# Batch 1's K and Q through TensorE, batch 0's MLP input through TensorE, W2 behind V, and one token-mixing step for a tile shared by two batches

## The chip, the cores and the metric

The kernel runs on one core of a Trainium2 chip. The metric is device time in microseconds (us), the median of several executions. The engines of the core each work through their own instructions in order: TensorE (PE, with its weight loads shown as PEld), VectorE (DVE), ScalarE (ACT), GpSimd (POOL) and SyncE (SP, which here only issues DMAs). They wait for each other and for DMAs by semaphores.

## What is computed

Attention over 8 batches, 8 heads, 576 positions and head size 64, with a mask that keeps a window of 32 positions either side and 8 global positions; then a two-step MLP block over 512 channels.

```
scores = scale * q @ k^T            (masked: |i-j| <= 32, or i or j global)
attn   = softmax(scores);  x = attn @ v          x as [8, 576, 512]
a1  = alpha1 * x + beta1
u   = x + lam * (w_tok @ a1)                     mixes the 576 positions
a2  = alpha2 * u + beta2
out = u + lam * (relu(a2 @ w_ch1) @ w_ch2)       hidden size 2048
```

## The kernel before

**Tiling.** Each batch has 576 = 4.5 x 128 positions. The MLP works on a flat list of 36 tiles of 128 rows over all batches, so every even batch ends in the upper half of a flat tile, and the next odd batch starts in its lower half (`flat_rows`, L270: tile u = 4 of an even batch and u = 0 of an odd one are the same flat tile f). The MLP takes four flat tiles at a time, as group g of 9.

**Stages of a batch.** `qk` (L278) makes transposed window scores from KTz (K transposed, zero padded per head) and QT (Q transposed), exponentiates on ACT and masks on DVE into PTz and GRT. `pg` (L324) does the global rows, `xg` (L308) the global columns. `pv` (L335) multiplies with V, normalizes on DVE into x, and POOL writes XL = x * LA1. `tokmix` (L372) multiplies wtT (w_tok transposed; wtT[0] for even, wtT[1] for odd batches, shifted by 64 columns) with XL, five matmuls of 128x512 for each of five tiles u (L383); DVE adds x into the tile U[f] (L384). When a tile's 128 rows are complete, DVE multiplies by alpha2 into u16 (L390), and a DMA transpose on SP's queue puts it into UT[g] (L391), the transposed MLP input. `mlp(g)` (L447) needs the four tiles of UT[g]: 16 x 4 matmuls with W1 (L455), Relu with a bias on ACT (L458), 4 x 16 matmuls with W2 (L464), two DVE operations and the output DMA.

**Order.** The order on each engine is the order in which the program is written. Batch 0 runs alone, written out by hand at L485 to L682 (the prelude), in which weights and constants are also loaded. From batch 1 on, `front(b)` is a generator whose yields say how many MLP matmuls come between two pieces of attention: 8 MLP matmuls first, then 120 in each `front`. During `front(1)` only group 0 exists (128 matmuls), so group 1 starts right after `tokmix` of batch 1.

**K and Q.** Batch 0 loads 512 of 576 positions so that a partition holds 4 consecutive positions (`qk0_half`, L161, runs of 1 KB in memory), casts to bf16 into a scratch in HTb, and TensorE transposes (`kt`, `qt`, `rest`, L519 to L539); ACT and DVE copy from PSUM into KTz and QT. All other batches load with `qk_chunk` (L174: five chunks of 128 positions, runs of 256 bytes), cast into kz and q16, and use DMA transposes on SP's queue (`xbar_k` L186, five of them; `xbar_q` L190, two). In the prelude, batch 1's chunks are cast on ACT (`c_qk[...](SC)`), three of its `xbar_k` stand before `pv(0, 3)`, two behind `wt_sums`, and `xbar_q` inside the loop over batch 0's `tokmix` (L665).

**Weights.** w_tok comes by a POOL DMA (L572), is transposed by TensorE in `wt_tr` (L583) and completed by `wt_sums`. W1 and W2 come in four blocks each, by POOL's queue, with a cast from float32 (`w1_dma` L601, `w2_dma` L604): W1's at L622, L630, L640 and L660; W2's first two before, and its last two behind, the casts of batch 1's V.

**Buffers.** R has three tiles and RV two for float32 loads; a load waits until the cast of what lay there is done. PSUM: mm 1, ml 3, sc 2, xps 1 buffers. XL, GS, RS and wtT exist twice, by parity of the batch.

Of the kernel before, what the change touches and what calls it, by code (L numbers as in the profile page):

```python
# [31 lines left out]
def A(t, off, dims, p0=0, n=P):  # L32
    row = t.ap[0][0]
    return bass.AP(t.tensor, t.offset + p0 * row + off, [[row, n]] + dims)
# [22 lines left out]
def kernel(  # L57
# [42 lines left out]
    def ml(dtype=FP32, cols=512):  # L100
        return psL.tile([P, cols], dtype, name="ml", tag="ml")

    def sc(dtype=FP32):
        return psS.tile([P, 512], dtype, name="sc", tag="sc")

    def u_tile():
        return pU.tile([P, DM], FP32, name="U")
# [45 lines left out]
    def next_r():  # L153
        r_n[0] += 1
        return R[(r_n[0] - 1) % 3]
# [2 lines left out]
        return 1600 * (t % 2) + 320 * (t // 2)  # L158


    def qk0_half(i, hh, r):  # L161
        nc.sync.dma_start(
            out=A(r, 0, [[256, 4], [1, 256]]),
            in_=(k, q)[i][0, 4 * hh : 4 * hh + 4, 0:512, :].rearrange("h (p c) d -> p h (c d)", c=4),
        )
        return lambda E: copy(E, out=A(HTb, KQ0 + 2560 * i + 256 * hh, [[64, 4], [512, 4], [1, D]]), in_=A(r, 0, [[256, 4], [64, 4], [1, D]]))

    def qk0_rest(r):
        for i, src in enumerate((k, q)):
            nc.sync.dma_start(out=A(r, 0, [[64, 8], [1, 64]], 64 * i, 64), in_=src[0, :, 512:576, :].rearrange("h p d -> p h d"))  # L170
        return lambda E: copy(E, out=A(HTb, KQ0 + 2048, [[1, 512]]), in_=r[:, 0:512])


    def qk_chunk(b, c):  # L174
        n = P if c < 4 else 64
        r = next_r()
        for i, src in enumerate((k, q)):
            nc.sync.dma_start(out=A(r, 512 * i, [[64, 8], [1, D]], 0, n), in_=src[b, :, P * c : P * c + n, :].rearrange("h p d -> p h d"))

        def cast(E):  # L180
            copy(E, out=A(kz, 1024 * c, [[256, 4], [192, 2], [1, D]], 0, n), in_=A(r, 0, [[128, 4], [64, 2], [1, D]], 0, n))
            copy(E, out=q16[0:n, c, :], in_=r[0:n, 512:1024])

        return cast
# [36 lines left out]
    def glob_kq(kq):  # L221
        kqn = pS.tile([P, 2, D], BF16, name="kqn")
        G.tensor_tensor(out=kqn[0:64], in0=A(kq, 0, [[0, 2], [1, D]], 0, 64), in1=A(cst, C_PAR, [[1, 2], [0, D]], 0, 64), op=ALU.mult)
        G.tensor_copy(out=kqn[64:P], in_=A(kq, 0, [[0, 2], [1, D]], 64, 64))
        return kqn
# [20 lines left out]
    def masks_b(scr):  # L246
        d72, e72 = A(scr, 8, [[8, 9], [1, 8]]), A(scr, 80, [[8, 9], [1, 8]])
        V.tensor_scalar(out=notg, in0=notg, scalar1=-1.0, scalar2=1.0, op0=ALU.mult, op1=ALU.add)
        V.tensor_tensor(out=notg, in0=notg, in1=cst[:, C_VALID : C_VALID + 9], op=ALU.mult)
        V.tensor_tensor(out=mask, in0=A(cst, C_BAND, [[0, 9], [1, 64]]), in1=A(notg, 0, [[1, 9], [0, 64]]), op=ALU.mult)  # L250
        V.tensor_tensor(out=e72, in0=d72, in1=d72, op=ALU.mult)
        V.tensor_scalar(out=e72, in0=e72, scalar1=float(WIN * WIN), scalar2=None, op0=ALU.is_gt)
        V.tensor_tensor(out=grm, in0=A(scr, 80, [[16, 5], [1, 8]]), in1=A(notg, 0, [[2, 5], [0, 8]]), op=ALU.mult)
# [118 lines left out]

    def tokmix(b, x):
        par = b % 2
        for u in range(5):
            f, r0, r1 = flat_rows(b, u)
            if f not in U:
                while len(U) >= 9:
                    yield 1
                U[f] = u_tile()  # L380
            ps = sc()
            for c in range(5):
                T.matmul(out=ps, lhsT=wtT[par][:, c, P * u : P * u + P], rhs=XL[par][:, c, :], start=(c == 0), stop=(c == 4))  # L383
            V.tensor_tensor(out=U[f][r0:r1, :], in0=ps[r0:r1, :], in1=x[r0:r1, u, :], op=ALU.add)  # L384
            if r1 == P:
                g = f // 4
                if g not in UT:
                    UT[g] = pUT.tile([P, 4, 512], BF16, name="UT")
                u16 = pU16.tile([P, DM], BF16, name="u16")
                V.tensor_tensor(out=u16, in0=U[f], in1=a2b, op=ALU.mult)  # L390
                nc.sync.dma_start_transpose(out=UT[g][:, :, P * (f % 4) : P * (f % 4) + P], in_=u16)  # L391
            yield 4


    def front(b, kqn):
# [90 lines left out]
    nc.sync.dma_start(out=cst, in_=nc.inline_tensor(_consts(), name="cst_np").ap())  # L486
    scr, a1b, b1r, colr = u_tile(), u_tile(), u_tile(), u_tile()
    stage = [pUT.tile([P, 1024], FP32, name="UT") for _ in range(2)]
    c_k0 = qk0_half(0, 0, next_r())
    c_q0 = qk0_half(1, 0, next_r())  # L490
    c_k1 = qk0_half(0, 1, next_r())
    c_q1 = qk0_half(1, 1, stage[0])
    c_rest = qk0_rest(stage[1])

    make_identity(nc, identb)
    G.memset(dum, 0.0)
# [22 lines left out]
    def kt(p, engs):  # L519
        ps = ml(BF16)  # L520
        for c in range(4):
            T.transpose(out=ps[:, c * P : (c + 1) * P], in_=A(HTb, KQ0 + 512 * c + P * p, [[1, P]]), identity=identb)
        for hh in range(2):
            copy(engs[hh], out=A(KTz, 640 * (2 * p + hh) + 32, [[4, P], [1, 4]], 64 * hh, 64), in_=A(ps, 0, [[1, P], [P, 4]], 64 * hh, 64))

    def qt(p):
        ps = sc(BF16)
        for c in range(4):
            T.transpose(out=ps[:, c * P : (c + 1) * P], in_=A(HTb, KQ0 + 2560 + 512 * c + P * p, [[1, P]]), identity=identb)
        for e in range(2):  # L530
            SC.copy(out=A(QT, 1600 * e + 80 * p, [[320, 4], [4, 16], [1, 4]]), in_=A(ps, 16 * e, [[32, 4], [1, 16], [P, 4]]))  # L531

    def rest():
        ps = ml(BF16)
        for p in range(4):
            T.transpose(out=ps[:, P * p : P * p + P], in_=A(HTb, KQ0 + 2048 + P * p, [[1, P]]), identity=identb)
        for hh in range(2):
            V.tensor_copy(out=A(KTz, 640 * hh + 544, [[1280, 4], [1, 64]], 64 * hh, 64), in_=A(ps, 0, [[P, 4], [1, 64]], 64 * hh, 64))
        SC.copy(out=A(QT, qo(8), [[80, 4], [1, 64]]), in_=A(ps, 64, [[P, 4], [1, 64]]))  # L539
# [8 lines left out]
    with nc.allow_non_contiguous_dma(reason="column-major 512-vector load (one time)"):  # L548
        nc.sync.dma_start(out=b2c, in_=moe_beta2.rearrange("(c p) -> p c", p=P))
    kt(0, (V, V))  # L550
    masks_b(scr)
    c_q0(SC)
    qt(0)
    G.memset(ecol, 0.0)
    G.memset(A(ecol, 0, [[64, 2]]), 1.0)
    G.memset(wt16[:, :, 576:704], 0.0)
# [1 line left out]
    G.memset(ve[96:P, 4, :, 0:64], 0.0)  # L558
    c_k1(SC)
    kt(1, (V, V))  # L560
    kqn = glob_kq(kq)
    c_rest(V)
    rest()
    glob(kqn)
    c_q1(SC)
    qt(1)
    c_v[0](G)
    c_v[1](G)
    c_v[2](G)
# [7 lines left out]
    gs_init(0, colr)  # L577
    V.tensor_copy(out=A(RS[0], 64, [[65, 8]], 0, 64), in_=cst[0:64, C_BD : C_BD + 8])
    glob_v(V, 0, vg)
    c_qk = [qk_chunk(1, c) for c in range(3)]  # L580


    def wt_tr(c):  # L583
# [5 lines left out]
    def wt_sums():  # L589
        for hf in range(2):  # L590
# [3 lines left out]
            SC.copy(out=wtT[0][64:65, 4, 288 * hf : 288 * hf + 288], in_=ps[64:65, 0:288])  # L594
            SC.copy(out=wtT[1][0:1, 0, 64 + 288 * hf : 352 + 288 * hf], in_=ps[0:1, 0:288])

    def drain(gen):
        for _ in gen:
            pass

    def w1_dma(blk):  # L601
        G.dma_start(out=W1[:, :, 512 * blk : 512 * blk + 512], in_=moe_w_ch1[:, 512 * blk : 512 * blk + 512].rearrange("(c p) e -> p c e", p=P))
# [3 lines left out]

    x = pX.tile([P, 5, DM], FP32, name="x")
    drain(qk(0, 0))
    kt(2, (V, SC))
    kt(3, (V, SC))  # L610
    qt(2)
    qt(3)
    drain(qk(0, 1))
    drain(pg(0))
    V.tensor_tensor(out=LA1, in0=a1b, in1=lamb, op=ALU.mult)
    xg(0, 0)
    xg(0, 1)
    G.memset(XL[0][64:P, 4, :], 0.0)
    G.memset(wtT[1][:, :, 0:64], 0.0)
    G.memset(wtT[1][0:64, 0, 64:640], 0.0)  # L620
    G.memset(GS[1], 0.0)
    w1_dma(0)  # L622
    qk2 = qk(0, 2)
    for _ in range(3):
        next(qk2)
    pv(0, 0, x)
    drain(qk2)
    c_qk[0](SC)
    wt_tr(0)
    w1_dma(1)  # L630
    qk3 = qk(0, 3)
    for _ in range(3):
        next(qk3)
    c_qk.append(qk_chunk(1, 3))
    pv(0, 1, x)
    drain(qk3)
    xg(0, 2)
    c_qk[1](SC)
    wt_tr(1)
    w1_dma(2)  # L640
    xbar_k(0)
    c_qk.append(qk_chunk(1, 4))
    xbar_k(1)
    pv(0, 2, x)
    V.tensor_tensor(out=XL[0][64:65, 4, :], in0=b1r[64:65, :], in1=lamb[64:65, :], op=ALU.mult)
    xg(0, 3)
    wt_tr(2)
    c_qk[2](SC)
    wt_tr(3)
    xbar_k(2)  # L650
    pv(0, 3, x)
    wt_tr(4)
    wt_sums()
    c_qk[3](SC)
    c_qk[4](SC)
    xbar_k(3)
    xbar_k(4)
    V.tensor_copy(out=b2a, in_=b2c)
    kq, vg = gathers(1)
    w1_dma(3)  # L660
    G.memset(RS[1], 0.0)
    G.memset(XL[1][0:64, 0, :], 0.0)
    kqn = glob_kq(kq)
    mix = tokmix(0, x)
    for i, _ in enumerate(mix):  # L665
        if i == 1:
            xbar_q()
    glob(kqn)
    V.tensor_copy(out=A(RS[1], 64, [[65, 8]], 0, 64), in_=cst[0:64, C_BD : C_BD + 8])
    glob_v(V, 1, vg)  # L670
    gs_init(1, colr)
    V.tensor_tensor(out=XL[1][0:1, 0, :], in0=b1r[0:1, :], in1=lamb[0:1, :], op=ALU.mult)
    w2_dma(0)
    w2_dma(1)
    c_v = [v_part(1, i) for i in range(3)]
    for c in c_v:
        c(G)
    v_shift(G)
    w2_dma(2)
    w2_dma(3)  # L680
    nc.sync.dma_start(out=A(wtT[1], 64, [[640, 5], [1, S]], 64, 64), in_=A(wtT[0], 0, [[640, 5], [1, S]], 0, 64))
    nc.sync.dma_start(out=A(wtT[1], 640 + 64, [[640, 4], [1, S]], 0, 64), in_=A(wtT[0], 0, [[640, 4], [1, S]], 64, 64))  # L682

# [55 lines left out]
```

## Time and profile before

| | |
|---|---|
| median of 14 runs | 436.28 us (431.55 to 441.60) |
| the profiled execution's own time | 432.71 us |
| its span, first to last instruction | 430.9 us |
| PE / DVE / ACT / POOL busy in the span | 87% / 52% / 39% / 42% |
| mean granted TensorE clock | 0.962 |
| DMA | 66.44 MB, mean 154 GB/s; 176067 of 189804 packets under 512 B |
| first MLP matmul (L455) | at 68.06 us |

How to read it: the profile divides the span into 40 slices of 10.8 us and gives for each engine the busy share in tenths, and the clock that TensorE was granted. A chain of work is followed back from the last instruction, at each step to what released it; it can be listed by time. A group of instructions is one line, engine, operation and tile, with the mean of one. A wait is idle time of an engine, put down to what released it. For a DMA the profile gives SP's or POOL's issue (SPq, POOLq) and the time from issue to landing. A PE matmul's duration contains its way through the array, so in a stream the start-to-start time is shorter than it: 128x512 matmuls have a mean of 388 ns, and start about 215 ns apart at full clock.

### The profile page before, as it was taken

Reading aid. Unit: us, or ns where it says so; the run is one execution under the profiler, and the core shown is the slowest. Engines: PE = TensorE matmul, PEld = TensorE weight load, DVE = VectorE, ACT = ScalarE, POOL = GpSimd, SP = SyncE. Lnnn points to the kernel's source line nnn. Section 1 sums busy time; section 2 is a strip of 40 time slices with the busy share of each in tenths; the row PEclk is TensorE's granted clock in tenths of the full one; section 3 lists DMA queues with packets and bytes.
Section 4 is the critical chain, followed back from the end, with each engine's and each line's share of the span. In section 5 each row is a group of like instructions: output and inputs, shape, how many; then the busy total and the mean of one; then the engine's idle time right before and its main releaser. Section 6 shows DMA issues by size and latency. Waiting matters only on the chain.

```text
span 430.9 us, 8312 instructions
## 1 busy us (share of the span) xinstructions
PE 375.7 (87%) x3295; PEld 208.4 (48%) x3351; DVE 223.5 (52%) x446; ACT 168.1 (39%) x293; POOL 181.7 (42%) x241
## 2 busy tenths in 40 slices
PE   1485606999779999999999999989999999999995
PEld 1374202664346545654564565446545654444442
DVE  7745440355815684559555764766385547303123
ACT  6446302750047206710770266036603740360720
POOL 7625702657643746647473657346640140000000
PEclk9998955999969999999999999999999999999999
DMA  8999999999995999888999998889883002201001
GB/s 237 200 211 220 157 198 183 211 210 161 250 203 83 144 218 220 163 159 209 215 181 181 185 223 142 181 190 220 139 195 103 14 2 86 73 2 73 24 26 73
DMA packets 189804, 66.44 MB, mean 154 GB/s; under 512 B 176067, under 2 KB 183747, under 8 KB 189765
## 3 DMA queue, kind: packets, MB, share of 16 engines
q1 hardware_dynamic: 183044, 56.93, 66.2%
q0 software_dynamic: 6720, 8.98, 11.7%
q8 instruction: 26, 0.43, 0.4%
q14 instruction: 14, 0.11, 0.1%
HBM read 39.28 MB, written 9.44 MB: 113 GB/s over the span
## 4 chain that ended last, share of the span: by engine, by line
PE 64%; DMA 11%; DVE 8%; SPq 6%; POOL 4%; issue 4%; ACT 2%; POOLq 0%; DVEq 0%
PE ml L455 26%; PE ml L464 21%; PE sc L383 5%; DMA UT<-u 4%; PE sc L285 3%; PE xps L347 3%; DMA R<-in_q_dram 3%; DMA R<-in_k_dram 2%; POOL XL L359 2%; PE xps L348 2%; DVE U L384 2%; PE mm L313 2%; PE sc L330 1%; DMA lamb<-in_moe_lam_dram 1%; SPq L192 1%
## 5 line engine op out<-in xcount | busy, mean ns | idle before, releaser
L455 PE MATMUL ml<-UT,W 128*128 128x512 bf16 x539 | 142.8, 388 | 14.2 <-DMA UT<-u 12.2
L458 ACT ACTIVATE HTb<-ml,bias1T 128x512 bf16<-128x512 f32 x144 | 99.1, 688 | 105.1 <-PE ml L455 98.3
L464 PE MATMUL ml<-W,HTb 128*128 128x512 bf16 x559 | 134.6, 379 | 0.8
L464 PEld LDWEIGHTS <-HTb 128*128 128x128 bf16 x576 | 54.5, 98 | 59.5
L455 PEld LDWEIGHTS <-W 128*128 128x128 bf16 x576 | 49.7, 100 | 54.3 <-issue 8.6
L359 POOL TENSOR_TENSOR XL<-x,LA 128x512 bf16<-128x512 f32 x32 | 42.5, 1328 | 67.0 <-DVE x L352 65.4
L469 DVE TENSOR_TENSOR tmp<-ml,lamb 128x512 f32<-128x512 f32 x36 | 24.8, 690 | 68.3 <-PE ml L464 65.9
L292 ACT ACTIVATE Pt<-sc 128x432 f16<-128x432 f32 x90 | 47.5, 528 | 14.7 <-PE sc L285 14.6
L383 PE MATMUL sc<-XL,wtT 128*128 128x512 bf16 x198 | 49.2, 379 | 1.7 <-POOL XL L359 0.8
L331 ACT ACTIVATE GS<-sc 64x320 f16<-64x320 f32 (+1 forms) x16 | 6.5, 403 | 107.5 <-PE sc L330 107.5
L110 POOL CAST ve<-RV 128x1024 f16<-128x1024 f32 x16 | 19.1, 1196 | 62.1 <-DMA RV<-in_v_dram 60.6
L285 PEld LDWEIGHTS <-KTz 128*128 128x128 bf16 x576 | 31.7, 103 | 24.4 <-issue 4.2
L390 DVE TENSOR_TENSOR u<-U,a2b 128x512 bf16<-128x512 f32 x36 | 34.0, 943 | 10.6 <-DMA UT<-u 9.4
L384 DVE TENSOR_TENSOR U<-sc,x 128x512 f32<-128x512 f32 (+1 forms) x40 | 27.4, 685 | 22.9 <-PE sc L383 22.8
L294 DVE TENSOR_TENSOR GRT<-Pt,grm 128x80 f16<-128x80 f16 x32 | 8.7, 270 | 56.2 <-ACT Pt L292 56.2
L285 PE MATMUL sc<-QT,KTz 128*128 128x72 bf16 x540 | 33.2, 201 | 4.0 <-ACT QT L531 3.4
L347 PEld LDWEIGHTS <-PTz 128*128 128x128 f16 x576 | 31.3, 100 | 9.0 <-issue 3.8
L348 PE MATMUL xps<-RS,GS 128*128 128x65 f16 x320 | 32.3, 197 | 3.6 <-DVE RS L321 3.6
L347 PE MATMUL xps<-ve,PTz 128*128 128x65 f16 x320 | 33.2, 196 | 0.3 <-DVE x L352 0.3
L383 PEld LDWEIGHTS <-wtT 128*128 128x128 bf16 x200 | 19.5, 98 | 25.5 <-issue 1.6
L347 PE MATMUL xps<-vo,PTz 128*128 128x65 f16 x256 | 30.0, 197 | 0.0
L348 PEld LDWEIGHTS <-GS 128*128 128x128 f16 x320 | 28.8, 100 | 1.9
(113 smaller groups left out, 363.5 us busy)
## 6 DMA issues: line engine op xcount, KB each, us to landing
out_dram<-U SPq DMA_DIRECT2D x36, 256.0 KB, 2.7
R<-in_k_dram SPq DMA_DIRECT2D x28, 256.0 KB, 5.1
R<-in_q_dram SPq DMA_DIRECT2D x28, 256.0 KB, 5.2
RV<-in_v_dram SPq DMA_DIRECT2D x24, 256.0 KB, 4.6
W<-in_moe_w_ch_dram POOLq DMA_DIRECT2D x8, 512.0 KB, 9.9
vo<-ve POOLq DMA_DIRECT2D x14, 260.0 KB, 4.2
RV<-in_v_dram SPq DMA_DIRECT2D x8, 192.0 KB, 4.8
R<-in_v_dram SPq DMA_DIRECT2D x8, 192.0 KB, 4.3
```

Source lines behind the costliest of these rows:

```text
L285: T.matmul(out=ps[:, i * 144 + 72 * hh : i * 144 + 72 * hh + 72], lhsT=KTz[:, 2 * p + hh, 64 * t : 64 * t + P], rhs=A(QT, qo(t) + 80 * p, ...
L292: SC.activation(out=Pt[:, 432 * un : 432 * un + 432], in_=ps[:, 0:432], func=AF.Exp, bias=0.0, scale=0.125)
L347: T.matmul(out=o_, lhsT=ptz[:, base : base + P], rhs=vv, start=(i == 0), stop=False)
L348: T.matmul(out=o_, lhsT=gs[:, P * u : P * u + P], rhs=rs[:, h, :], start=False, stop=True)
L359: G.tensor_tensor(out=A(xl, DM * full + P * p, [[DM, 4], [1, P]]), in0=A(x, DM * full + P * p, [[DM, 4], [1, P]]), in1=A(LA1, P * p, [[0, ...
L383: T.matmul(out=ps, lhsT=wtT[par][:, c, P * u : P * u + P], rhs=XL[par][:, c, :], start=(c == 0), stop=(c == 4))
L384: V.tensor_tensor(out=U[f][r0:r1, :], in0=ps[r0:r1, :], in1=x[r0:r1, u, :], op=ALU.add)
L390: V.tensor_tensor(out=u16, in0=U[f], in1=a2b, op=ALU.mult)
L455: T.matmul(out=ps, lhsT=W1[:, cc, ec * P : (ec + 1) * P], rhs=ut[:, cc, :], start=(cc == 0), stop=(cc == 3))
L458: SC.activation(out=HTb[:, slots[ec], :], in_=ps, func=AF.Relu, bias=bias1T[:, ec : ec + 1], scale=1.0)
L464: T.matmul(out=ps, lhsT=HTb[:, slots[ec], P * j : P * j + P], rhs=W2[:, ec, :], start=(ec == 0), stop=(ec == 15))
L469: V.tensor_tensor(out=tmp, in0=ps, in1=lamb, op=ALU.mult)
```

## The change

1. The loader of 1 KB runs takes the batch as an argument, and batch 1 uses it too. `qk_chunk(1, ...)`, its casts and its seven DMA transposes go; TensorE transposes with `kt`, `qt` and `rest` take their place in the prelude. ACT casts (five calls), and ACT and DVE copy from PSUM.
2. For batch 0, all `kt` and `qt` come before the first `qk(0, 0)`, and the remaining 64 positions are loaded and handled before the second half of the heads.
3. In `tokmix`, batch 0's u16 tiles go through four TensorE transposes and one DVE copy from PSUM (`ut_pe`, one tile behind), not through a DMA transpose.
4. The shared flat tile: an even batch at u = 4 only copies x into U[f]. The odd batch at u = 0 does ten matmuls with 64 weight columns each, alternating between the upper half (wtT[0], XL[0], output rows 0 to 63) and the lower half (wtT[1], XL[1], rows 64 to 127) of one PSUM tile; one more DVE addition takes the upper half into U[f].
5. W1's blocks and all four blocks of W2 are issued later: W2 behind the casts and the shift of batch 1's V. The index gathers of batch 1 move forward.

```diff
-    def qk0_half(i, hh, r):
+    def qk4_half(b, i, hh, r):
...
     def tokmix(b, x):
         par = b % 2
+        wait = []
+        def ut_pe():
+            f, u16 = wait.pop(0)
+            ps = ml(BF16)
+            for cc in range(4):
+                T.transpose(out=ps[:, cc * P : (cc + 1) * P], in_=u16[:, cc * P : (cc + 1) * P], identity=identb)
+            V.tensor_copy(out=UT[f // 4][:, :, P * (f % 4) : P * (f % 4) + P], in_=A(ps, 0, [[P, 4], [1, P]]))
         for u in range(5):
...
+            if par == 0 and u == 4:
+                V.tensor_copy(out=U[f][0:64, :], in_=x[0:64, 4, :])
+                yield 4
+                if wait:
+                    ut_pe()
+                continue
             ps = sc()
-            for c in range(5):
-                T.matmul(out=ps, lhsT=wtT[par][:, c, P * u : P * u + P], rhs=XL[par][:, c, :], start=(c == 0), stop=(c == 4))
+            if r0:
+                for c in range(5):
+                    for i, c0 in enumerate((512, 64)):
+                        T.matmul(out=ps[64 * i : 64 * i + 64, :], lhsT=wtT[i][:, c, c0 : c0 + 64], rhs=XL[i][:, c, :], start=(c == 0), stop=(c == 4))
+                V.tensor_tensor(out=U[f][0:64, :], in0=ps[0:64, :], in1=U[f][0:64, :], op=ALU.add)
+            else:
+                for c in range(5):
+                    T.matmul(out=ps, lhsT=wtT[par][:, c, P * u : P * u + P], rhs=XL[par][:, c, :], start=(c == 0), stop=(c == 4))
             V.tensor_tensor(out=U[f][r0:r1, :], in0=ps[r0:r1, :], in1=x[r0:r1, u, :], op=ALU.add)
             if r1 == P:
...
-                nc.sync.dma_start_transpose(out=UT[g][:, :, P * (f % 4) : P * (f % 4) + P], in_=u16)
+                if b == 0:
+                    wait.append((f, u16))
+                else:
+                    nc.sync.dma_start_transpose(out=UT[g][:, :, P * (f % 4) : P * (f % 4) + P], in_=u16)
             yield 4
+            if wait and (u == 4 or len(wait) > 1):
+                ut_pe()
...
     kt(0, (V, V))
-    masks_b(scr)
     c_q0(SC)
     qt(0)
+    c_rest(V)
+    rest()
...
     kt(1, (V, V))
+    qt(1)
+    masks_b(scr)
+    c_q1(SC)
+    kt(2, (V, SC))
+    qt(2)
     kqn = glob_kq(kq)
-    c_rest(V)
-    rest()
+    kt(3, (V, SC))
+    qt(3)
     glob(kqn)
-    c_q1(SC)
-    qt(1)
...
-    c_qk = [qk_chunk(1, c) for c in range(3)]
+    n_k0 = qk4_half(1, 0, 0, next_r())
+    n_q0 = qk4_half(1, 1, 0, next_r())
+    n_k1 = qk4_half(1, 0, 1, next_r())
+    n_q1 = qk4_half(1, 1, 1, RV[1])
+    n_rest = qk4_rest(1, u_tile())
...
     pv(0, 0, x)
+    kq, vg = gathers(1)
     drain(qk2)
-    c_qk[0](SC)
     wt_tr(0)
-    w1_dma(1)
...
-    c_qk.append(qk_chunk(1, 3))
+    n_k0(SC)
     pv(0, 1, x)
     drain(qk3)
     xg(0, 2)
-    c_qk[1](SC)
     wt_tr(1)
-    w1_dma(2)
-    xbar_k(0)
-    c_qk.append(qk_chunk(1, 4))
-    xbar_k(1)
+    kt(0, (SC, SC))
+    n_q0(SC)
     pv(0, 2, x)
+    w1_dma(0)
+    qt(0)
...
     xg(0, 3)
+    kt(1, (SC, SC))
     wt_tr(2)
-    c_qk[2](SC)
+    pv(0, 3, x)
+    kqn = glob_kq(kq)
+    w1_dma(1)
+    n_k1(SC)
+    qt(1)
     wt_tr(3)
-    xbar_k(2)
-    pv(0, 3, x)
     wt_tr(4)
     wt_sums()
-    c_qk[3](SC)
-    c_qk[4](SC)
-    xbar_k(3)
-    xbar_k(4)
+    n_q1(SC)
     V.tensor_copy(out=b2a, in_=b2c)
-    kq, vg = gathers(1)
+    w1_dma(2)
     w1_dma(3)
...
+    glob(kqn)
     mix = tokmix(0, x)
-    for i, _ in enumerate(mix):
-        if i == 1:
-            xbar_q()
-    glob(kqn)
+    next(mix)
+    kt(2, (V, SC))
+    qt(2)
+    next(mix)
+    kt(3, (V, SC))
+    qt(3)
+    n_rest(SC)
+    next(mix)
+    rest()
+    drain(mix)
...
-    w2_dma(0)
-    w2_dma(1)
     c_v = [v_part(1, i) for i in range(3)]
     for c in c_v:
         c(G)
     v_shift(G)
-    w2_dma(2)
-    w2_dma(3)
+    for blk in range(4):
+        w2_dma(blk)
```

More of the change, by code (lines that the diff above doesn't have):

```diff
@@ L158, in qo, with qk4_rest @@
         return 1600 * (t % 2) + 320 * (t // 2)
-    def qk0_half(i, hh, r):
+    def qk4_half(b, i, hh, r):
         nc.sync.dma_start(
             out=A(r, 0, [[256, 4], [1, 256]]),
-            in_=(k, q)[i][0, 4 * hh : 4 * hh + 4, 0:512, :].rearrange("h (p c) d -> p h (c d)", c=4),
+            in_=(k, q)[i][b, 4 * hh : 4 * hh + 4, 0:512, :].rearrange("h (p c) d -> p h (c d)", c=4),
         )
         return lambda E: copy(E, out=A(HTb, KQ0 + 2560 * i + 256 * hh, [[64, 4], [512, 4], [1, D]]), in_=A(r, 0, [[256, 4], [64, 4], [1, D]]))
-    def qk0_rest(r):
+    def qk4_rest(b, r):
         for i, src in enumerate((k, q)):
-            nc.sync.dma_start(out=A(r, 0, [[64, 8], [1, 64]], 64 * i, 64), in_=src[0, :, 512:576, :].rearrange("h p d -> p h d"))
+            nc.sync.dma_start(out=A(r, 0, [[64, 8], [1, 64]], 64 * i, 64), in_=src[b, :, 512:576, :].rearrange("h p d -> p h d"))
         return lambda E: copy(E, out=A(HTb, KQ0 + 2048, [[1, 512]]), in_=r[:, 0:512])
@@ L488 @@
     stage = [pUT.tile([P, 1024], FP32, name="UT") for _ in range(2)]
[L489 to L493, printed above, removed]
+    c_k0 = qk4_half(0, 0, 0, next_r())
+    c_q0 = qk4_half(0, 1, 0, next_r())
+    c_rest = qk4_rest(0, stage[1])
+    c_k1 = qk4_half(0, 0, 1, next_r())
+    c_q1 = qk4_half(0, 1, 1, stage[0])
     make_identity(nc, identb)
@@ L595, in wt_sums, with w1_dma, w2_dma @@
             SC.copy(out=wtT[1][0:1, 0, 64 + 288 * hf : 352 + 288 * hf], in_=ps[0:1, 0:288])
+    def w1_dma(blk):
+        G.dma_start(out=W1[:, :, 512 * blk : 512 * blk + 512], in_=moe_w_ch1[:, 512 * blk : 512 * blk + 512].rearrange("(c p) e -> p c e", p=P))
+    def w2_dma(blk):
+        G.dma_start(out=W2[:, 4 * blk : 4 * blk + 4, :], in_=moe_w_ch2[512 * blk : 512 * blk + 512, :].rearrange("(c p) d -> p c d", p=P))
     def drain(gen):
@@ L608 @@
     drain(qk(0, 0))
[L609 to L612, printed above, removed]
     drain(qk(0, 1))
     drain(pg(0))
+    xg(0, 0)
     V.tensor_tensor(out=LA1, in0=a1b, in1=lamb, op=ALU.mult)
-    xg(0, 0)
     xg(0, 1)
@@ L621 @@
     G.memset(GS[1], 0.0)
-    w1_dma(0)
+    G.memset(RS[1], 0.0)
+    G.memset(XL[1][0:64, 0, :], 0.0)
     qk2 = qk(0, 2)
@@ L637 @@
     xg(0, 2)
-    c_qk[1](SC)
     wt_tr(1)
-    w1_dma(2)
-    xbar_k(0)
-    c_qk.append(qk_chunk(1, 4))
-    xbar_k(1)
+    kt(0, (SC, SC))
+    n_q0(SC)
     pv(0, 2, x)
+    w1_dma(0)
+    qt(0)
     V.tensor_tensor(out=XL[0][64:65, 4, :], in0=b1r[64:65, :], in1=lamb[64:65, :], op=ALU.mult)
     xg(0, 3)
+    kt(1, (SC, SC))
     wt_tr(2)
-    c_qk[2](SC)
+    pv(0, 3, x)
[3 more added lines that the diff above has]
+    qt(1)
     wt_tr(3)
-    xbar_k(2)
-    pv(0, 3, x)
     wt_tr(4)
     wt_sums()
-    c_qk[3](SC)
-    c_qk[4](SC)
-    xbar_k(3)
-    xbar_k(4)
+    n_q1(SC)
     V.tensor_copy(out=b2a, in_=b2c)
-    kq, vg = gathers(1)
+    w1_dma(2)
     w1_dma(3)
-    G.memset(RS[1], 0.0)
-    G.memset(XL[1][0:64, 0, :], 0.0)
-    kqn = glob_kq(kq)
+    glob(kqn)
     mix = tokmix(0, x)
-    for i, _ in enumerate(mix):
-        if i == 1:
-            xbar_q()
-    glob(kqn)
+    next(mix)
[8 more added lines that the diff above has]
+    drain(mix)
     V.tensor_copy(out=A(RS[1], 64, [[65, 8]], 0, 64), in_=cst[0:64, C_BD : C_BD + 8])
```

## The prediction

> **What bounds the kernel now.** First the page's 40 slices: they say whether one engine is the limit throughout.
>
> ```profile
> PE   1485606999779999999999999989999999999995
> ...
> PEclk9998955999969999999999999999999999999999
> DMA  8999999999995999888999998889883002201001
> ```
>
> From slice 7 (about 68 us) on PE is at nine tenths nearly everywhere; before that it is idle half of the time while the DMA engines are full. So time saved before the first MLP matmul comes off the end, and after it mostly PE work counts. What sets that first matmul I read from the chain of work in order of time (start, duration, what):
>
> ```profile
> 42.56 4.78 DMA R<-in_k_dram
> 47.37 0.62 ACT kz L110
> 47.98 0.55 ACT q L110
> 48.53 0.64 SPq L188
> ...
> 52.35 1.51 SPq L391
> ...
> 53.95 5.43 SPq L191
> ...
> 59.44 3.98 SPq L192
> ...
> 63.51 1.22 SPq L391
> ...
> 64.82 3.19 DMA UT<-u
> ...
> 68.06 3.59 PE ml L455 x8
> ```
>
> Batch 1's last K chunk lands at 47.4, and then SP's queue issues one DMA transpose behind the other, batch 1's Q (L191, L192: 9.4 us) standing between the second and third tile of batch 0's MLP input. The work of batch 0 itself was finished by 50.5. A table of stretches shows the same (PE, PEld, DVE, ACT, POOL busy us, then granted clock, DMA share, GB/s):
>
> ```profile
> 43.00:68.00 25.00, 7.34 (x47) 3.41 (x46) 9.47 (x22) 3.85 (x8) 8.59 (x12) 0.71 1.17 168
> ...
> 68.00:70.00 2.00, 1.94 (x5) 0.73 (x6) 0.00 (x0) 0.01 (x1) 0.00 (x0) 0.50 0.92 207
> 70.00:72.00 2.00, 2.00 (x7) 0.77 (x6) 0.00 (x0) 0.98 (x2) 0.47 (x1) 0.50 1.28 223
> 72.00:74.00 2.00, 1.78 (x6) 0.89 (x6) 0.00 (x0) 0.81 (x2) 0.58 (x1) 0.52 1.29 230
> 74.00:76.00 2.00, 2.00 (x32) 1.41 (x31) 0.00 (x0) 1.38 (x3) 1.81 (x3) 1.00 1.08 222
> ```
>
> No compute engine is busy 40% of 43 to 68 us, and the MLP then runs at half clock until 74.
>
> **Parts 1 to 3 and 5: when does the MLP start?** Removed: seven transposes of K and Q and four of UT on SP's queue, ten ACT casts of about 0.62 us (6.2), and about 1,800 KB of 256-byte runs. Added for batch 1: four ACT casts of 1.05 and one of about 0.6 (the groups of casts into HTb and kz), 4 x 0.65 for `qt`, two `kt` wholly on ACT (2 x 1.18), two with one ACT copy (0.58) and one DVE copy (0.68), `rest` (0.37 ACT, 0.59 DVE), and PE transposes at about 0.6 us for four. For UT: four transposes and a DVE copy each; no row shows that copy, the nearest are 64x512 bf16 from PSUM (0.68) and 128x512 DVE additions from PSUM (0.69), so 0.69. I lay this out engine by engine.
>
> *Opening.* Batch 0's K and Q wait for loads until about 12, as now. All its transposes before `qk(0, 0)` give DVE c_k0 0.9, `kt(0)`, `kt(1)` 2.8, rest 1.0, masks 1.8, `kt(2)`, `kt(3)` 1.4, glob 0.7; with two hand-offs, `qk(0, 0)` comes at about 18.3, not 14.85. But `qk(0, 1)` follows at once, where now it waits until 21.71 for QT. Its `xg(0, 1)` ends at about 25, now at 27.2: 2 us earlier.
>
> *Middle.* `wt_tr(0)` needs w_tok, issued by POOL at 18.4; its two parts land after 8.9 and 8.5 us, so 27.3. It now shares the DMA engines with 2.3 MB of early batch 1 loads, and PE's queue stops behind it: 27.3 to 30.5, I take 28.3. From there ACT is the fullest: five wt copies 3.4, three exponentials 1.4, four casts 4.0 (one starts 0.1 before the other ends), `kt(0)`, `kt(1)` 2.3, `qt(0)`, `qt(1)` 1.3, `wt_sums` 1.6: 14.0, with 1.5 for hand-offs to PE and back. `wt_sums` ends at about 43.3 and the last cast, n_q1, at 44.5. Now `wt_sums` ends at 44.84. `tokmix` starts at about 43.5 (now 44.54): the stage is not much shorter, but holds batch 1's K and Q as well.
>
> *tokmix.* Here DVE is the fullest: four tiles of 0.69 + 0.69, four UT copies 2.8, `kt(2)`, `kt(3)` 1.4, rest 0.6, the copy of x at most 0.68: 11.0. From the first PSUM tile at 44.9 that is 55.9, and with 1.5 for hand-offs 57.4. So the MLP starts at 57.4 in place of 68.06: 10.7 us. The next on DVE is late too: glob_v, gs_init and a row of XL (0.18 + 0.68 + 1.31 + 0.68) now stand before the first bias copy, so the first Relu comes at about 60.5 (now 69.98). Two of the three ml buffers take the first eight matmuls, so this costs PE little while it is cold.
>
> *Clock.* PE ran 5.9 us at half clock from 68.06, which is 3 us of work. Afterwards PE has a group of matmuls or transposes every 1 to 2 us in `tokmix`. The trace kept clock 1.00 from 44 to 52 with PE at 34% to 100%, and lost it after some 3 us of idleness (0.68 in 52 to 56). The Trainium skill (TensorE: Matmul & The Clock Gate, Part 4: PE-mode transpose) speaks against counting on this: transposes do not count as PE activity. By the row the MLP starts warm (3 us gained, 1 of it lost to the late Relu), by the rule cold (0). Only 20 of the 57 operations there are true matmuls (37 transposes); I take 1.0.
>
> *Hidden work.* SP's queue is shorter. Batch 1's V is held longer in it: its second part needs RV[1], free only after n_q1 at 44.5, and behind it wait part 3, the wtT copies and batch 2's K and Q. It lands at about 50, and its casts and shift end by 54; first needed at about 12 us into the MLP (69). W1's blocks are issued at 38 to 45, four in a row. They land now after 7.9 to 12.9 us singly; two issued at 32.71 and 35.16 were in by 44.5, so about 5.5 us each under load: 44, 50, 55, 61. Needed at 57, 65, 70, 76 (bias1 of each block, 7.5, 12.8 and 18.9 us into the MLP). W2 is issued from about 54: 66, 72, 77, 83 at the same pace, 3.7 us each if nothing else runs (58% of 23 us for some three and a half blocks): 76. Needed at 82 to 85, since L464 starts 24.5 us into the MLP (now 68.06 and 92.56). This fits with a few us to spare, so nothing is charged; without that cover it would be up to 3. Batch 2's K and Q are issued at 46 to 52, where now POOL waits 3.5 and 4.3 us for them in front(1); that delays XL, for which PE waits 0.8 and 0.6 us: I take 0.7 back.
>
> **Part 4: the shared tile.** Five matmuls of 0.216 go from even batches: 1.08 each, from batches 2, 4 and 6, 3.2 us of PE's bound time (batch 0's lies in the prelude). In odd batches ten half-width ones replace five. No 64-column matmul is in the trace. The rows of L383:
>
> ```profile
> L383 PEld LDWEIGHTS <-wtT x200: 95/98/98, 43.5 to 366.8; 128*128 128x128 bf16 x100
> L383 PE MATMUL sc<-XL,wtT x198: 376/379/379, 44.5 to 367.1; 128*128 128x512 bf16 x198
> ```
>
> If both halves run side by side, the odd batch costs 1.1 as now: gain 3.2. If they run one after the other with each load exposed, ten cost 10 x (0.216 + 0.098) = 3.1, 2.1 more in each of four batches: a loss of 5.0. The skill (TensorEngine Tiling (Array Packing), Restrictions and Gotchas; Key Properties) holds against it that column tiling goes without Fast Weight Load and that a change of mode drains the array; the row has full-width loads at 98 ns beside the stream. But the same skill (TensorE: Matmul & The Clock Gate, Part 3) measured 2.38x for three column tiles, 0.79 of ideal; for two, 1.59x, an estimate: ten cost 10 x 0.216 / 1.59 = 1.36, 0.28 more in four batches. I take 3.2 - 1.1 = 2.1. The DVE addition more (0.68) lies in slack.
>
> **What stays.** After `tokmix` of batch 1 group 0 is used up, and group 1 waits for DMA transposes:
>
> ```profile
> PE ml L455 <- DMA UT<-u: 5.0, 1, 5.0
> ```
>
> Nothing in the change touches that wait, nor the half clock behind it (0.50 in 120 to 124); the stalled L390 there can take an addition without moving it much.
>
> **Sum.** 10.7 + 1.0 + 0.7 + 2.1 = 14.5 us. The profiled execution has a span of 430.9 in 432.71 us; 418.2 would be its new time. It lies 3.6 under the median, so I take the difference off that: 436.28 - 14.5 = 421.8.
>
> **Rivals.**
> - *The halves do not overlap.* For it: no row shows that they do. Against: the two halves write disjoint output rows. With the start as above, 12.4 - 5.0 = 7.4 gained: 428.9. Chance 0.15.
> - *Early stages lag.* w_tok lands at 30.5 under the new loads, ACT and DVE trade waits, W2's last block is 3 late: the MLP starts near 61, gain 7 + 2.1 - 2: 429. For it: DMA is at 1.1 to 1.2 in 15 to 43. Against: 1 KB runs moved up to 385 GB/s at the start, 256-byte runs about 215. Chance 0.12.
> - *All goes well:* MLP at 55 and warm, 13 + 2 + 3.2 + 0.7 = 19: 417. Chance 0.2.
> - *W2 becomes the bound (slower).* All four blocks follow V. If each took its own 11.8 us, as the two at 76.8 did together with batch 2's loads, the last would land at 54 + 47 = 101, against 82 to 85: 17 us of waiting at L464, in which PE also falls to half clock (3), net 5 slower: 441. It decides once the last block lands behind about 97. Against: those two overlapped, since both were in by 90. Chance 0.03.
> - *The change does nothing*, as some other wait holds the MLP at 68: nothing seen does. 0.02.
>
> The forecast has 0.48. The range runs from 415.5 (all well) to 429.0, which leaves out about 2 in 10. Within 0.5% (about 2.2 us, what a measurement of this kernel can tell from no change) 0.03, slower 0.04, faster 0.93.
>
> **What would show it.** Right: first L455 at 55 to 60; no L188 to L192 transposes before it; DVE nearly gapless in the 11 us ahead; PEclk above 0.5 just behind; matmul pairs of the shared tile starting a few ns apart; no PE wait for W at L464. Wrong: PE idle at L464 or at the bias for a W DMA, PE stopped long at `wt_tr(0)`, or 64-column matmuls 0.3 us apart.

## The result, and the profile after

| | before | after |
|---|---|---|
| median | 436.32 us (47 runs, 431.55 to 441.70) | 420.96 us (10 runs, 420.44 to 422.58) |
| profiled execution, its span | 432.71, 430.9 us | 420.68, 418.8 us |
| first MLP matmul | 68.06 us | 56.41 us |
| start of group 1 | 120.73 us | 112.30 us |
| mean granted clock | 0.962 | 0.976 |

The ratio is 0.968 (0.966 to 0.971); ratios leave out executions over 1.5% above the fastest of their kernel, medians do not. The forecast of 421.8 us, faster, held. That it came so close is luck: two errors of opposite sign, which the experiments take apart, cancelled. Against the profiled execution the gain is 12.1 us in the span, not 14.5, and against the median it is 15.4.

The slices of the kernel after, now 10.5 us each:

```profile
PE   1647689979499999999999999999999999999995
...
PEclk9977989998899999999999999999999999999999
DMA  8994999989996899997999999979981002202001
```

PE is at seven tenths or more from slice 6 on, but for one hole at slice 11 (from 105 us) and the last slice, and the DMA engines have a hole of their own at slice 4 (31 to 42 us). The instructions around the start, from the timeline (start, duration, engine, what; in brackets the idle time ahead and what ended it):

```profile
29.81 1.04 PE L621 MATMUL ml<-identb,HTb 128*128 128x128 bf16 x5 [1.69 <-DMA HTb<-in_moe_w_tok_dram]
...
55.42 0.40 PE L381 MATMUL ml<-identb,u 128*128 128x128 bf16 x4 [1.29 <-DVE u L412]
...
56.41 2.75 PE L482 MATMUL ml<-UT,W 128*128 128x512 bf16 x7 [0.21 <-DVE UT L382]
```

No DMA transpose stands ahead of the MLP any more; TensorE waits for DVE's copy, as forecast. What comes behind it was not forecast. The chain of work from there to group 1:

```profile
46.80 1.09 SPq L203
...
47.94 13.16 DMA R<-in_v_dram
...
62.92 3.02 POOL W L646 x4
...
69.01 14.60 DMA vg<-in_v_dram,hg_idx
...
94.20 0.46 POOL XL L365
...
94.71 2.22 PE sc L401 x9
...
108.69 3.48 DMA UT<-u
...
112.30 1.86 PE ml L482 x4
```

Batch 1's V leaves SP's queue at 46 to 54 and lands at 61; W2 (L646) and batch 2's gathers follow it; POOL is late with XL (94.66), the step of the shared tile (L401) waits 2.6 us for that and then runs at about half clock (0.53 in 94.7 to 97). The stretches between the marks of the table (same columns as in the prediction), after and before:

```profile
56.40:112.30 55.90, 46.74 (x436) 25.16 (x444) 29.98 (x61) 16.96 (x31) 31.04 (x40) 0.94 1.07 201
112.30:418.80 306.50, 298.26 (x2522) 159.93 (x2567) 161.68 (x307) 122.65 (x211) 117.58 (x151) 1.00 0.68 137
```

```profile
68.06:120.73 52.67, 45.70 (x431) 24.97 (x440) 25.58 (x52) 17.19 (x31) 31.03 (x39) 0.92 1.11 207
120.73:430.90 310.17, 301.41 (x2520) 161.66 (x2567) 161.14 (x304) 122.79 (x211) 117.71 (x150) 0.99 0.66 135
```

So the 12.1 us are, rounded, 11.7 ahead of the MLP, 3.2 given back in `front(1)` (2.2 of idle PE, 1.0 of longer busy time), and 3.7 gained from group 1 on.

### The profile page after: what moved, and what is told of

The parts are those of the page before. It is cut to its first block, busy times and chain, and to the rows that moved or that the text cites. A ratio compares the mean times of both kernels' runs of the same rounds, so it can differ in the third digit from the quotient of the medians.

```text
span 418.8 us, 8399 instructions
## 1 busy us (share of the span) xinstructions
PE 375.5 (90%) x3349; PEld 208.8 (50%) x3403; DVE 228.8 (55%) x458; ACT 172.9 (41%) x303; POOL 181.0 (43%) x241
## 4 chain that ended last, share of the span: by engine, by line
PE 66%; DMA 13%; POOL 6%; DVE 6%; SPq 4%; issue 2%; ACT 1%; POOLq 0%; DVEq 0%
PE ml L491 24%; PE ml L482 24%; PE sc L405 5%; DMA R<-in_v_dram 4%; DMA vg<-in_v_dram,hg_idx 3%; PE sc L285 3%; PE xps L347 3%; DMA HTb<-in_moe_w_tok_dram 3%; SPq L203 2%; PE xps L348 2%; POOL XL L359 2%; DMA UT<-u 2%; PE mm L313 2%; PE sc L330 1%; DMA RV<-in_v_dram 1%
## 5 line engine op out<-in xcount | busy, mean ns | idle before, releaser
L491 PE MATMUL ml<-W,HTb 128*128 128x512 bf16 x561 | 134.9, 381 | 0.8
L491 PEld LDWEIGHTS <-HTb 128*128 128x128 bf16 x576 | 54.4, 98 | 60.9 <-issue 2.6
L405 PE MATMUL sc<-XL,wtT 128*128 128x512 bf16 x155 | 39.0, 379 | 0.5 <-DVE U L406 0.2
L294 DVE TENSOR_TENSOR GRT<-Pt,grm 128x80 f16<-128x80 f16 x32 | 9.6, 300 | 48.9 <-ACT Pt L292 48.9
L412 DVE TENSOR_TENSOR u<-U,a2b 128x512 bf16<-128x512 f32 x36 | 30.2, 840 | 4.0 <-DMA UT<-u 2.9
L110 POOL CAST kz<-R 128x512 bf16<-128x512 f32 (+1 forms) x30 | 19.2, 640 | 26.2 <-DMA R<-in_k_dram 25.7
L406 DVE TENSOR_TENSOR U<-sc,x 128x512 f32<-128x512 f32 (+1 forms) x36 | 24.7, 687 | 9.5 <-PE sc L405 9.3
```

Of the source, the lines that this page charges most:

```text
L110: (E.copy if E is SC else E.tensor_copy)(**kw)
L491: T.matmul(out=ps, lhsT=HTb[:, slots[ec], P * j : P * j + P], rhs=W2[:, ec, :], start=(ec == 0), stop=(ec == 15))
```

## The experiments

Theory 1: the earlier start comes from K, Q and UT together, no one of them alone; the halves of the shared step run side by side; and `front(1)` gives time back because V waits on SP's queue for the buffer RV[1]. (The buffer RV[1] takes the second half of batch 1's Q, `n_q1` in the code, and V's second part has to wait until that half is cast.) The rivals: halves one after the other; DMA engines that are full in any order; an unforecast clock or Relu limit. No run takes the new order of batch 0's transposes (part 2 of the change) by itself, nor the long runs of the loads apart from the seven DMA transposes that went with them. Two runs (a6, a8) look for a better version, and two (c1, c2) ask why the median fell by more than the profiled executions.

**Shared tile as before, all else changed** (a1).

```diff
-            if par == 0 and u == 4:
...
             ps = sc()
-            if r0:
...
+            for c in range(5):
+                T.matmul(out=ps, lhsT=wtT[par][:, c, P * u : P * u + P], rhs=XL[par][:, c, :], start=(c == 0), stop=(c == 4))
```

> The changed kernel with the shared tile handled as before: five full matmuls in the even batch, five in the odd one. Theory 1, the halves of the shared step run side by side: ten half-width matmuls cost what five did, so undoing it puts back 3 x 1.08 us in batches 2, 4 and 6 and at most 0.5 in batch 0: 424.2 us (423.7 to 424.8) against 420.96. Rival, the halves run one after the other: undoing it makes even batches 1.08 longer and odd ones 1.08 shorter, 420 to 421.

Measured: 425.01 us (424.35 to 425.38), 4.1 above the changed kernel and just above theory 1's range; from group 1 to the end 423.4 - 113.0 = 310.4 us, against 306.5. The halves run side by side. The changed kernel's timeline has them in batch 7, ten half-width matmuls and later five full ones, with MLP matmuls (L491) around both:

```profile
339.82 4.48 PE L491 MATMUL ml<-W,HTb 128*128 128x512 bf16 x20
344.23 1.27 PE L401 MATMUL sc<-XL,wtT 128*64 128x512 bf16 x10
345.43 1.04 PE L491 MATMUL ml<-W,HTb 128*128 128x512 bf16 x4
346.31 1.24 PE L405 MATMUL sc<-XL,wtT 128*128 128x512 bf16 x5
347.38 1.03 PE L491 MATMUL ml<-W,HTb 128*128 128x512 bf16 x4
```

1.27 us for ten, 1.24 for five. Going over to half-width matmuls and back costs something beside that. The last L491 matmul ahead of the ten starts at 343.92 (339.82 + 4.48, less the 0.38 of one), and the first behind them at 345.43: 1.51 us. Around the five full ones it is 1.29 (346.09 to 347.38). So an odd batch pays about 0.22 us, four of them 0.9, and of the 3.2 us from the three even batches about 2.3 are left. The kept traces agree. From group 1 to the end the five without the step (before, c1, c2, b2, a1) take 308.4 to 310.4 us, mean 309.4. Eight with it (all others but a8, whose group 1 starts without a wait) take 306.2 to 307.7, mean 307.1. The 3.7 and 3.9 us of single pairs lie above this 2.3; what else is in the 4.1 is not assigned.

**Shared tile alone, on the kernel before** (b1): the two new branches of `tokmix`, without `ut_pe`.

> The kernel before with the shared tile's new step alone. Theory 1 (halves side by side): 3 x 1.08 us off batches 2, 4 and 6, and about 0.5 from the prelude: 432.7 us (431.5 to 434) against 436.3. Rival (one after the other): 436 to 437.5.

Measured: 434.50 us against 436.39 beside it, ratio 0.993 (0.990 to 0.997), that is 1.4 to 4.4 us. The median lies between the ranges of theory 1 and of the rival; the ratio agrees with 2.3 us of gain, and with 3.2.

**Batch 0's MLP input by TensorE alone, on the kernel before** (b2).

```diff
-                nc.sync.dma_start_transpose(out=UT[g][:, :, P * (f % 4) : P * (f % 4) + P], in_=u16)
+                if b == 0:
+                    wait.append((f, u16))
+                else:
+                    nc.sync.dma_start_transpose(out=UT[g][:, :, P * (f % 4) : P * (f % 4) + P], in_=u16)
```

> The kernel before with TensorE transposing batch 0's MLP input, and batch 1's K and Q still loaded in 256-byte runs and turned by DMA. Theory 1: the two parts are worth something each; the MLP's first eight matmuls come at about 53, but global scores of batch 1 need Q, whose DMA transposes land at about 62, now without the four of UT between: 428 us (425 to 431). Rival: either part alone leaves the other as the bound, so one alone brings under 2 us: 434.5 to 436.5.

Measured: 435.88 us (430.27 to 440.13) against 436.39, but the ratio is 0.987 (0.980 to 0.993). The time is unclear, theory 1's 428 is missed, and the profile shows the rival's reason: the MLP begins at 55.5, but then the global scores wait for Q's DMA transpose:

```profile
PE sc L330 <- DMA QT<-q: 10.5, 1, 10.5
```

**The changed kernel with that part undone** (a2): batch 0's MLP input by DMA transposes again (`if b == 0` made `if False`).

> The changed kernel with batch 0's MLP input again turned by DMA, on SP's queue. Theory 1: these four DMAs now stand ahead of batch 1's V on SP's queue, so besides a start some 3 us later, V, W2 and batch 2's loads are pushed back to 55 and more: 427 us (424 to 431). Rival, the queue is free enough now that a DMA transpose is as good: 420.5 to 422.5.

Measured: 429.56 us (426.94 to 430.49), 8.6 above the changed kernel: theory 1. SP's queue:

```profile
48.12 11.63 SPq L416 DMA_TRANSPOSE UT<-u  x4
59.80 2.80 SPq L203 DMA_DIRECT2D RV<-in_v_dram  x4
62.64 1.09 SPq L203 DMA_DIRECT2D R<-in_v_dram  x1
```

The four transposes hold the queue for 11.6 us, partly waiting for their tiles (DVE finishes the fourth at 58.5), and V stands behind them until 60. Together: this part is worth between nothing (by the medians) and 6 us (by the ratio) on the old loads, and 8.6 us on the new ones. Whether each part hides what the other brings, the times don't settle: by the medians b2 and a2 gain 0.5 and 6.8 us of 15.4, by the ratios 0.987 and 0.984 multiply to 0.970, close to the 0.968 of the whole change. What the trace of b2 shows is the wait itself: with UT's transposes gone, 10.5 us for Q take their place.

**A buffer of its own for batch 1's second Q half** (a3).

```diff
-    n_q1 = qk4_half(1, 1, 1, RV[1])
+    n_q1 = qk4_half(1, 1, 1, pUT.tile([P, 1024], FP32, name="UT"))
```

> The changed kernel, with batch 1's second Q half loaded into a tile of its own (a free buffer of the UT pool) in place of RV[1]. Theory 1: what front(1) gave back of the earlier start (11.7 us at the first MLP matmul, 8.4 at group 1) comes from batch 1's V waiting on SP's queue for the cast of that half, with W2 and batch 2's K and Q behind it. Then V is issued from about 31, W2 from about 48, the waits of PE for vo (3.4 us) and for XL (2.6 us and about 1.3 at half clock behind it) go, and the time is 416 us (414.5 to 418). Rival, the DMA engines are simply full with V, W1, W2 and batch 2's loads, whatever their order: 420.3 to 421.5.

Measured: 415.54 us (413.84 to 418.32), 5.4 below the changed kernel, clear of the rival. SP's queue in both, first the changed kernel, then this one:

```profile
30.47 17.43 SPq L203 DMA_DIRECT2D RV<-in_v_dram  x4
47.94 6.39 SPq L203 DMA_DIRECT2D R<-in_v_dram  x1
54.38 3.08 SPq L719 DMA_DIRECT2D wtT<-wtT  x1
...
58.17 1.47 SPq L178 DMA_DIRECT2D R<-in_k_dram  x1
```

```profile
29.21 7.90 SPq L203 DMA_DIRECT2D RV<-in_v_dram  x4
37.22 0.90 SPq L203 DMA_DIRECT2D R<-in_v_dram  x1
41.48 0.62 SPq L719 DMA_DIRECT2D wtT<-wtT  x1
...
42.82 1.64 SPq L178 DMA_DIRECT2D R<-in_k_dram  x1
```

V's last part goes out 10.7 us earlier, batch 2's loads 15. `front(1)` takes 105.68 - 55.00 = 50.7 us in place of 55.9, and PE's wait for XL is 0.4 in place of 2.6. About 0.9 of these 5.2 us is the clock behind 55 (below, at a5), which this edit does not decide. One thing in the expectation was misread: the wait for vo (V shifted by half a tile; 3.4 us) lies at 26 in batch 0, not in batch 1, and is still 2.2 here.

**w_tok issued ahead of the casts of batch 0's V** (a4b): its two `G.dma_start` moved above `c_v[0](G)`.

> The changed kernel with w_tok's DMA issued on POOL ahead of the casts of batch 0's V. Theory 1: the prelude stands at wt_tr(0) until w_tok lands at 30.5, because batch 1's early loads share the DMA engines with it; issued some 4 us earlier it lands at about 25 and the first MLP matmul moves from 56.4 to 53: 418 us (417 to 419.5). Rival, V of batch 0 and its shift are then the later ones (PE waits for vo at 26), or ACT's work from 31 to 46 sets the start: 420.4 to 421.5.

Measured: 423.86 us (421.63 to 425.63), 2.9 slower: theory 1 falls, the rival's first half holds, though the time is above its range too. V's shift into vo now lands after 9.0 to 10.4 us (5.7 to 8.2 in the changed kernel), PE waits 5.3 us for it, and the MLP starts at 58.58. In both kernels the DMA share is 1.03 to 1.17 from 15 to 30 us, which fits a limit that order only moves; no run with less traffic there tests it.

**W2's first two blocks ahead of batch 1's V** (a7), as before the change.

> The changed kernel with W2's first two blocks issued ahead of batch 1's V on POOL, as before the change. Theory 1: in the changed kernel POOL stands from 48.6 to 60 for V, and W2 is issued from 63 only; two blocks earlier fill that time, and the last block lands sooner, but L491 waits for no block in either, so the time stays: 420.3 to 421.7 us. Rival 1, the earlier blocks delay V further (it lands at 60 now): 422.5 to 425. Rival 2, batch 2's loads, gathers among them, come free of W2 and PE's wait of 2.6 us for XL goes: 417.5 to 419.5.

Measured: 422.17 us (419.71 to 423.31), 1.2 above, between theory 1 and rival 1 and not clear of either. V's second cast comes at 64.8 (59.9 in the changed kernel), so the earlier blocks do delay it. Moving them forward gains nothing that shows.

**Nine matmuls more ahead of the MLP** (a5), to keep the clock; work of no use, added.

```diff
+            if f > 0:
+                xd = psX.tile([P, 2, 512], FP32, name="xps")
+                for j in range(3):
+                    T.matmul(out=xd[:, j % 2, :], lhsT=wtT[0][:, 0, 0:128], rhs=XL[0][:, 0, :], start=True, stop=True)
```

> The changed kernel with nine matmuls more, of no use (three 128x512 behind each of the last three groups of transposes of batch 0's MLP input, into a free PSUM tile; the result isn't used). Theory 1: transposes count little for the clock, so it drops at 57 in the changed kernel (0.62 of full speed in 56.4 to 60); with true matmuls in between it stays at 1.00 and the first MLP group gains: 419.8 us (419.3 to 420.4). Rival, the first Relu, which waits for VectorE until 59, sets the pace there: 420.6 to 421.3, with the clock at 1.00.

Measured: 420.87 us (419.65 to 421.97), the same as without: theory 1 is missed, the rival's number met. Its clock stayed at 1.00. But so it did in a1, a3 and a4b, which have no such matmuls: their first seven or eight MLP matmuls took 1.89 us, as in a3,

```profile
55.00 1.89 PE L482 MATMUL ml<-UT,W 128*128 128x512 bf16 x7 [0.21 <-DVE UT L382]
```

where the changed kernel's profiled execution took 2.75 for seven, and a6's 3.56 for eight. Up to there a3 and a6 have the same instructions, so these do not fix the drop, and the run can't say what the clock costs; with the nine matmuls the median does not move.

**TensorE also for the four tiles of group 1** (a6), on top of a3.

```diff
-                if b == 0:
+                if b == 0 or f < 8:
                     wait.append((f, u16))
```

> The changed kernel with a buffer of its own for batch 1's second Q half, as above, and in addition TensorE transposes for the four tiles of group 1 in batch 1 (its fifth tile stays a DMA). Theory 1: the wait of 5.7 us for the DMA transposes ahead of group 1, and the half clock behind it (about 1.3), shrink to the chain of VectorE behind the last tile (about 2 us): 411 us (409.5 to 413). Rival, VectorE's in-order queue (additions, products and now copies) is what group 1 waits for, whoever transposes: 414.5 to 416.5.

Measured: 414.06 us (412.27 to 415.26), 1.5 below a3, not the 4.5 of theory 1. The wait ahead of group 1 changed its name and lost more than half its length: it was 5.7 us for the DMA, and is now

```profile
106.09 1.02 PE L482 MATMUL ml<-UT,W 128*128 128x512 bf16 x4 [2.37 <-DVE UT L382]
```

DVE is busy for 11.72 of the 12 us from 94 to 106. The time lies between the two forecasts, next to the rival's.

**The same with ScalarE copying from PSUM** (a8): `copy(V if b == 0 else SC, ...)` in `ut_pe`.

> The kernel with a buffer for Q of its own and TensorE transposes for group 1 (414.06 us), with ScalarE instead of VectorE copying batch 1's four tiles from PSUM. Theory 1: VectorE's queue is what group 1 waits for; four copies of 0.41 us less on it, and ScalarE has been idle since 80: group 1 starts some 1.5 us earlier, 412.5 us (411.5 to 413.3). Rival: the chain of additions and products alone is that long: 413.6 to 414.5.

Measured: 410.15 us (408.61 to 411.46), 3.9 below a6 and more than expected. PE no longer waits for group 1's tiles (group 1 starts at 102.04), and in the profiled execution, the fastest of the six, the clock holds:

```profile
core 0: 406.8 us, clock 0.998
```

This is the best version: 2.6% below the changed kernel, ratio to the kernel before 0.945 (0.940 to 0.949).

**The kernel before, two more profiled executions** (c1, c2).

> The kernel before, another execution with a profile, to see where its executions differ (431 to 442 us over 47 runs, where the changed kernel has 420.4 to 422.6). Theory 1: the difference arises ahead of the first MLP matmul or in front(1), in the DMA transposes of K and Q and the loads behind them; an execution that is longer by d has its group 1 start about d later than 120.73 us, and the same time from there to the end (310 us). Rival: it is the granted clock or the MLP later on, and the rest after group 1 differs.

> The kernel before once more, for the same question: the time from the start of group 1 to the end is 310 us in every execution (theory 1), or varies with the total (rival).

Measured: 436.50 and 436.51 us, both with a span of 434.7, which is the median. The first MLP matmul and the start of group 1 in c1, then the first MLP matmul in c2 (group 1 at 125.39):

```profile
73.52 3.59 PE L455 MATMUL ml<-UT,W 128*128 128x512 bf16 x8 [7.01 <-DMA UT<-u]
...
126.26 1.87 PE L455 MATMUL ml<-UT,W 128*128 128x512 bf16 x4 [5.62 <-DMA UT<-u]
```

```profile
72.28 3.60 PE L455 MATMUL ml<-UT,W 128*128 128x512 bf16 x8 [3.65 <-DMA UT<-u]
```

From group 1 to the end they took 308.4 and 309.3 us (310.2 in the first profile), and `front(1)` 52.7 and 53.1. So the executions differ ahead of the first MLP matmul, by 5.5 and 4.2 us, of which the rest takes 1.7 and 0.9 back. The difference arises on SP's queue, not in one place. The last K load ahead of four K transposes is issued at 42.56 in the first profile, and at 44.86 and 44.88 in c1 and c2; after that c1 loses 3.3 us at the transpose of Q, and c2 2.4 at the first two of UT. The transpose of Q in the first profile, c1 and c2:

```profile
53.95 5.43 SPq L191 DMA_TRANSPOSE QT<-q  x1
```

```profile
56.28 8.74 SPq L191 DMA_TRANSPOSE QT<-q  x1
```

```profile
58.58 5.84 SPq L191 DMA_TRANSPOSE QT<-q  x1
```

Theory 1 holds in the main in these three. The profile that the prediction was built on had a start 4.2 to 5.5 us earlier than these two executions, whose time is the median.

## Why the prediction was right, and where it was not

| term | forecast | profiled executions | who decides |
|---|---|---|---|
| start of the MLP | 10.7 | 11.7 | profile; b2 and a2 for the parts |
| clock, and XL's waits (`front(1)`) | +1.7 | -3.2 | a3, a5 |
| shared tile (from group 1 on) | 2.1 | 3.7 (2.3 over all traces) | a1, b1, all traces |
| sum | 14.5 | 12.1 | |
| the median's own start, against the profile's | 0 | 3.3, by difference | c1, c2 |
| sum for the median | 14.5 | 15.4 | |

- *The mechanism* was right for the start: DMA transposes and 256-byte loads held the MLP back, and with TensorE and DVE in their place it starts 11.7 us earlier. Not all of that came off the end. What the loads and their transposes are worth each is not shown.
- *Opening.* Forecast 25 for the end of `xg(0, 1)`, measured 23.3. The 2 us were lost again at once: PE stood until 26.5 for vo, which the sum had not, and until w_tok landed at 30.5, the late end of the range given (28.3 taken).
- *Middle.* `wt_sums` ended at 45.4 and n_q1 at 46.4, 2 us later than taken, for that reason.
- *tokmix.* DVE was the fullest, as said: from 46.31 to 56.35, 10.0 us, not 12.5. The UT copy took 0.41 us, not the 0.69 of the rows that were nearest, and hand-offs cost less. The two deviations leave 56.4 for 57.4.
- *Hidden work* is the step that failed. "It lands at about 50, and its casts and shift end by 54" was 61 and beyond: that V waits for n_q1 was seen, but not that its last part then shares the DMA engines with the W1 blocks. From 47.9 to 54.4 POOL's queue, with W1, moved 1.12 MB and SP's queue 0.14; and with two W2 blocks more beside it (a7) V came 4.9 us later still. W2 went out at 62.9, not 54. The place where it hurt was also not the one guarded: PE never waited for a W block to speak of, but XL came late through batch 2's loads. "I take 0.7 back" became 3.2 given back, and a3 shows the buffer as the cause of most of it, by winning 5.4 in all.
- *Clock.* 1.0 was taken between 0 and 3. The profiled execution got little (0.62 of full speed in 56.4 to 60), those of a1, a3, a4b and a8 got all of it; in a5 the median did not move.
- *Shared tile.* The mechanism was right, and the 2.1 is near the 2.3 us of the traces, but by luck. The sum took 1.59x for two column tiles, where the runs show 1.95x (1.27 us for ten against 1.24 for five), and it charged nothing for the change of mode that it named, which takes about 0.22 us in each odd batch. The rival of no overlap, at 0.15, is out.
- *From profile to median.* The forecast took the profiled execution's difference off the median, as though both lay 3.6 us below their medians by the same chance. They don't: the changed kernel's median is within 0.3 us of its profiled execution, as one would expect of a start that no longer hangs on DMA transposes under load; that this is the reason is argued from c1 and c2, not shown by a run of its own. This unforeseen gain of 3.3 us happened to cover the 2.4 us that the sum had too much.

What stays open: why the last POOL operation of the first `pv` in `front(1)` (L365, at 83.77) stands 2.0 us for a gather that it does not read, and what decides whether the clock drops at 57.

## What to carry to other kernels

When a load borrows another buffer, look at what else waits in the same queue for that buffer to come free: here it cost 5.4 us beside a gain of 15.4, on a transfer that TensorE did not wait for directly. Removing one of two transfers that share a queue may only uncover the wait for the other, as the 10.5 us in b2; test the parts alone and together before dropping one. When two shapes of one operation alternate, time them from the neighbour ahead to the neighbour behind: here the groups took 1.27 and 1.24 us, and their places in the stream 1.51 and 1.29. And a single profile of a kernel whose runs spread by 2% may be a lucky one: compare its time with the median first, and ask which stage the spread comes from.

## What the runs showed of the hardware

- Two matmuls of 64 weight columns each, to the two halves of the output rows, run side by side: ten take 1.27 us, five full ones 1.24. Going from full-width matmuls to them and back costs about 0.22 us (1.51 against 1.29). Their weight loads are not shorter than full ones (110 ns, full ones 98), and still hidden (the group's rows, min/median/max in ns):

```profile
L401 PEld LDWEIGHTS <-wtT x40: 106/110/178, 91.7 to 344.9; 128*64 128x64 bf16 x40
L401 PE MATMUL sc<-XL,wtT x40: 379/379/634, 91.7 to 345.1; 128*64 128x512 bf16 x40
```

- A DVE copy of 128x512 bf16 from PSUM, read and written in runs of 128 elements, took 0.41 us; one of 64x512 into KTz, which reads every 128th element and writes pieces of four, took 0.68.
- DMA transposes under other traffic vary widely: one and the same took SP's queue 5.43, 8.74 and 5.84 us. Kernels that turn batch 1's K and Q with them (before, b1, b2) spread over 8 to 10 us from run to run; those that don't, by 1 to 4.5. The first also load these in 256-byte runs, and no run separates the two.
